# Second stage in another order of frequencies, its first sums taken early, and tile sums begun 11 steps ahead

## The chip, the cores and the metric

One core of a Trainium2 chip runs the whole kernel. The metric is the device time of one execution in microseconds (us). TensorE (PE) does matrix products; VectorE (DVE), ScalarE (ACT) and GpSimd (POOL) do elementwise work; SyncE (SP) and ACT issue the DMA transfers. Each engine works through its own instructions in program order.

## What is computed

The reference is a long convolution with a gate, followed by a two-layer network:

```python
h_filt = (np.maximum(pos_emb @ w1, 0.0) @ w2) * np.exp(-0.01 * pos)[:, None]
u = x * v                                   # (2, 12480, 128)
y = irfft(rfft(u, 2 * S) * rfft(h_filt, 2 * S))[:, :S]
t = (x * y).reshape(2 * S, 128)             # 24960 rows
h = t @ w_in                                # 128 -> 2048
out = np.maximum(0.01 * h, h) @ w_out       # 2048 -> 128
```

## The kernel before, in words

The convolution of length 12480 is a transform of 98 x 128 points, split in two: 98 "frequencies" k on one axis, 128 on the other. Batch entry 0 is transformed before the network begins; batch entry 1 is transformed in small portions (the generator `conv`) between the network's matrix products, during its first half.

**First stage (L230 to L384).** The products over the 98-long axis, written to `scr1`. Its last turn also fills `bin0`, the input of the first chunk of the second stage: `early` takes what lies in `scr1` already, `direct` copies the last rows from one on-chip tile to another.

**Second stage (loop at L717).** 25 chunks of 4 frequencies (the last has 2, since 98 = 24 x 4 + 2), in rising order of frequency. For chunk c: `load_b` (L612) brings its input two chunks ahead; PE makes the spectrum of the filter (`hidden`, L693) and of the input (`fwd`, L121); DVE and POOL multiply them (`product`, L124); PE transforms back (`back_halves`, L149); `evac` (L705) copies the result to `ct` and ACT's queue stores it to the scratch `scr2[0]`. On the way the weights are converted and split, and `fetch_a` loads inputs for batch 1 at chunks 20 and 23 (`FETCH`).

**Tiles.** The result is taken up in 64 tiles (32 for each batch entry). For tile t, `load_gx` (L538) loads a matrix `gt` and the gate's inputs `xm`, and `load_c` (L556) loads `cin` from `scr2`: in column block j = 0 the frequencies 0 to 48, in j = 1 the frequencies 49 to 97, real part in the lower 49 partitions and imaginary part in the upper 49; block j = 2 holds the upper frequencies again with real and imaginary parts exchanged. `join` (L593) makes four sums and differences of these in `cp`, by two operations of 512 columns (`cq`, L601) and four of 256 (`cp`, L604). It runs on POOL for all tiles but tile 0, which runs on DVE. There is one `cp` buffer and one `cq` buffer. For tile 0, `load_c` runs when chunk 24 begins; the last two chunks' results are not read back from `scr2` but copied from `ct` straight into `cin` by `last_c` (L575), 20 small transfers in SP's queue.

**Network (loop at the end of the function).** 50 blocks of up to 512 columns, each with 16 steps, 800 steps in all. A step i is six matrix products: three in `m1` (L837 to L839) and three in `m2` (L869 to L871) of three steps earlier. Between steps stands what the table `steps` says. Tile t has a step `ends[t]`; `front(t)` (L804) is called twice: 3 steps before `ends[t]`, when PE multiplies `gt` with `cp` (L810, 16 products into `yp`), and at `ends[t]`, when PE transposes (L818), ACT rounds (`zh`, L829) and POOL subtracts (`zl`, L830). The block in which the tile's columns begin needs `zh` and `zl` in its first step. The due times come from

```python
for t in reversed(range(1, total)):
    e = min(e - 8, first[t] * NF - 3)
    ends[t] = e
```

so two tiles follow each other at 16 steps (tile 32 at 24, tile 1 stands at step 5) or, where two begin in the same block, at 8 steps. Worked out from this, 30 tiles come 8 steps after the one before; with t at least 36 there are 14 of them: 36, 37, 40, 41, 44, 45, 48, 49, 52, 53, 57, 58, 61 and 62; tile 33 is one more, and 15 lie between tile 2 and tile 31. Tiles 35, 39, 43, 47, 51, 56 and 60 come 16 steps after their predecessor and 8 before their successor; they reach `ends[t]` only three steps before their block begins. `join(t)` stands at `ends[t] - 8` in program order. `load_tile(t)` stands one step after `ends[t - 2]`. Batch 1's transform is spread over the steps up to 375.

Of the kernel before, what the change touches and what calls it, by code (L numbers as in the profile page):

```python
# [22 lines left out]
KC = 4  # L23
# [7 lines left out]
def tile_conv_mlp(ctx, tc, x, v, pos_emb, w1, w2, w_in, w_out, cf, cr, cg, cb, ci, cw, out):  # L31
# [6 lines left out]
    NCH = (NA + KC - 1) // KC  # L38
    R0 = 96
    L, H = slice(0, HB), slice(HB, 2 * HB)  # L40

    const = ctx.enter_context(tc.tile_pool(name="const", bufs=1))
    dram = ctx.enter_context(tc.tile_pool(name="dram", bufs=1, space=bass.MemoryType.DRAM))
# [163 lines left out]
    with tc.manual_schedule():  # L207
# [22 lines left out]
        with ExitStack() as st:  # L230
# [64 lines left out]

            NC0 = HB // MC
            DIR, EARLY = 1, 1
            load_pos(0)
            nc.vector.memset(w1bd, 0.0)
            for i in range(2):  # L300
# [10 lines left out]
            for c in range(NC0):  # L311
# [40 lines left out]
                def early():  # L352
                    for ri in range(2):
                        rows = slice(HB * ri, HB * ri + HB - DIR * MC)
                        nc.sync.dma_start(out=bin0[rows], in_=scr1[rows, :KC, :].rearrange("p k (s e) -> p k s e", s=2))
# [200 lines left out]
        def load_c(t):  # L556
            b, mp = divmod(t, NT)
            ci_t = mlp.tile([NA, 3, 2, 2, D], F32, tag="cin", name="cin")
            n = KH if t else (NCH - 2) * KC - KH
            ms = slice(2 * mp, 2 * mp + 2)  # L560
            for r in range(2):
                if t:
                    nc.sync.dma_start(out=ci_t[KH * r:KH * r + KH, 0:2].rearrange("k j m s d -> k j (m s d)"),
                                      in_=scr2[b][:, r, ms, :].rearrange("(j k) m e -> k j (m e)", j=2))
                else:
                    for j, k1 in ((0, KH), (1, n)):
                        nc.sync.dma_start(out=ci_t[KH * r:KH * r + k1, j].rearrange("k m s d -> k (m s d)"),
                                          in_=scr2[b][KH * j:KH * j + k1, r, ms, :].rearrange("k m e -> k (m e)"))
            nc.sync.dma_start(out=ci_t[KH:KH + n, 2].rearrange("k m s d -> k (m s d)"),
                              in_=scr2[b][KH:KH + n, 0, ms, :].rearrange("k m e -> k (m e)"))  # L570
            for i in range(2):
                nc.sync.dma_start(out=ci_t[:n, 2, :, i, :], in_=scr2[b][KH:KH + n, 1, ms, D - D * i:2 * D - D * i])
            ld[t] = (ci_t, *ld[t][1:])

        def last_c(ct, k0, n):  # L575

            ci_t = ld[0][0]
            k0 -= KH
            for r in range(2):
                for m in range(2):  # L580
                    src = ct[HB * r + m:HB * r + m + 1, :n]
                    nc.sync.dma_start(out=ci_t[KH * r + k0:KH * r + k0 + n, 1, m], in_=src)
                    if r == 0:
                        nc.sync.dma_start(out=ci_t[KH + k0:KH + k0 + n, 2, m], in_=src)
                    else:
                        for i in range(2):
                            nc.sync.dma_start(out=ci_t[k0:k0 + n, 2, m, i], in_=src[:, :, 1 - i])

        def load_tile(t):
            load_gx(t)  # L590
            load_c(t)

        def join(t):  # L593
# [11 lines left out]
            ld[t] = (cp, g, xt)  # L605

        with ExitStack() as st:
            sbb = st.enter_context(tc.tile_pool(name="sbb", bufs=2, reuse_waits="tile"))
# [65 lines left out]
            bins[0] = bin0  # L674
            load_b(1)
            wprep = weights()
            FETCH = [NCH - 5, NCH - 2]
            late = []
# [26 lines left out]
            def evac(c):  # L705
                ct = sbb.tile([128, KC, 2, D], F32, tag="ct", name="ct", bufs=2)
                k0, n = chunk(c)
                run(back_evac(dps.pop(c), ct, n))
                if c >= NCH - 2:
                    last_c(ct, k0, n)  # L710
                store_back(0, c, ct, nc.scalar)

            eh, dps = {}, {}
            ahead(A0)
            next(conv)
            hidden(0)
            for c in range(NCH):  # L717
                if c + 2 < NCH:
                    load_b(c + 2)
                if c == NCH - 2:  # L720
                    load_gx(0)
# [5 lines left out]
                if c == NCH - 2:  # L727
                    mult_a(1)
                for f in late:
                    f()  # L730
                late = []
                n = chunk(c)[1]
                t, es = bins.pop(c), eh.pop(c)
                hp = two("h")
                for ri in range(2):
                    for k in range(n):
                        i, j = 64 * (k % 2), ri * n // 2 + k // 2
                        nc.tensor.matmul(hp[k % 2][:, D * j:D * j + D], es[i:i + 64, k // 2, ri, :], w22[i:i + 64, :],
                                         start=True, stop=True)
                hs = sbb.tile([128, 2, KC // 2, 2, D], F32, tag="hs", name="hs", bufs=2)  # L740
                for i in range(2):
                    nc.scalar.copy(hs[:, :, :n // 2, i, :],
                                   hp[i][:, :n * D].rearrange("p (r j d) -> p r j d", r=2, d=D))
# [5 lines left out]
                if c + 1 < NCH:  # L749
                    hidden(c + 1)  # L750
# [4 lines left out]
                product(ab, up, hs, n * D, pins[c], nc.vector if c >= NCH - 2 else nc.gpsimd)  # L755
                if c >= 1:
                    dps[c - 1] = two("d")
                    back_halves(dps[c - 1], pins.pop(c - 1), c - 1)
                    evac(c - 1)
                for _ in range(2):  # L760
                    next(wprep, None)

# [3 lines left out]
                late.clear()  # L766

            ahead(A1)
            dps[NCH - 1] = two("d")
            back_halves(dps[NCH - 1], pins.pop(NCH - 1), NCH - 1)  # L770
            evac(NCH - 1)
            load_c(1)
            mult_a(2)
            ahead(A2)
# [170 lines left out]
        SLOTS = ends[NT] - 14  # L945
        done = AHEAD
        frt = front(0)
        join(0)
        next(frt)
        for _ in range(4 * A4):  # L950
            next(conv)
# [100 lines left out]
```

## Time and profile before

| | us |
|---|---|
| median of 3 runs (lowest, highest) | 1816.6 (1814.48, 1820.26) |
| the profiled execution's own time | 1818.74 |
| its span in the trace | 1816.9 |
| PE busy | 1695.9 (93% of the span) |
| DVE busy | 1122.9 (62%) |
| ACT busy | 986.7 (54%) |
| POOL busy | 793.7 (44%) |

The stages in this execution: first stage to about 168 us, second stage to about 345 us, then the start of the network; batch 1's transform runs beside the network until about 1140 us; from there to the end the network runs alone. A busy share says little by itself: what ended each idle time of PE, and the clock that PE was granted (PEclk, 1.00 is 2.4 GHz and 0.50 is 1.2 GHz), are to be read by stage.

### The profile page before, as it was taken

The page shows a single profiled execution, that of the slowest core. Times are in us where ns is not written, and L with a number is a line of the kernel's source. Part 1 is how long each engine was busy: PE and PEld are TensorE (multiplying, and loading weights), DVE is VectorE, ACT ScalarE, POOL GpSimd, SP SyncE. Part 2 cuts the span into 40 slices and gives each one's busy share as a digit, 9 for nine tenths or more (in the row PEclk, how much of TensorE's full clock was granted, in tenths as well). Part 3 has the DMA queues.
Part 4 walks back from the last instruction along what each step waited for, and adds up shares of the span by engine and source line. Part 5 has one row for each costly group of instructions (what it writes and reads, how often), then busy time and mean ns, then how long its engine had stood idle before and what let it go on. Part 6 is the DMA issues. An engine that isn't in the chain of part 4 may idle for free.

```text
span 1816.9 us, 27218 instructions
## 1 busy us (share of the span) xinstructions
PE 1695.9 (93%) x9185; PEld 1342.0 (74%) x9185; DVE 1122.9 (62%) x1702; ACT 986.7 (54%) x2006; POOL 793.7 (44%) x732
## 2 busy tenths in 40 slices
PE   6787999469999999999999999999999999999998
PEld 6786555268888877787887778777777777777778
DVE  4575788534554555554555554667767776777775
ACT  1222455224444466676666665556565666665656
POOL 3453112134424367776767673433424333425330
PEclk9889999769999999999999999999999999999999
DMA  9898999464666466565666622121211122111110
GB/s 226 241 282 251 320 324 336 163 169 135 196 179 186 121 163 174 151 182 147 184 162 172 169 77 88 54 66 42 68 55 53 53 60 68 47 50 58 52 31 19
DMA packets 165788, 253.26 MB, mean 139 GB/s; under 512 B 13730, under 2 KB 118458, under 8 KB 162576
## 3 DMA queue, kind: packets, MB, share of 16 engines
q1 hardware_dynamic: 145504, 225.82, 43.9%
q10 hardware_dynamic: 20144, 25.69, 4.0%
q8 instruction: 73, 1.20, 0.3%
q14 instruction: 67, 0.55, 0.1%
HBM read 167.94 MB, written 83.43 MB: 138 GB/s over the span
## 4 chain that ended last, share of the span: by engine, by line
PE 50%; DMA 13%; DVE 11%; issue 10%; POOL 8%; SPq 4%; ACT 3%; ACTq 0%; POOLq 0%; DVEq 0%
PE mh L837 6%; PE acc L870 6%; PE acc L871 6%; PE mh L839 6%; PE mh L838 6%; PE acc L869 6%; POOL cp L604 4%; DVE rl L854 3%; POOL cq L601 3%; PE cv L135 3%; PE yp L810 2%; DMA scr<-o 2%; PE cv L405 2%; DMA ft<-in_cf_dram 2%; DMA cin<-scr 2%
## 5 line engine op out<-in xcount | busy, mean ns | idle before, releaser
L844 DVE SCALAR_TENSOR_TENSOR rl<-mh,rh 128x512 fp32r<-128x512 f32 (+2 forms) x400 | 269.3, 677 | 323.5 <-ACT rh L843 320.4
L854 DVE TENSOR_TENSOR rl<-r,rh 128x512 fp32r<-128x512 f32 (+1 forms) x400 | 348.0, 885 | 148.5 <-ACT rh L853 141.6
L849 ACT ACTIVATE r<-mh 128x512 f32<-128x512 f32 (+1 forms) x400 | 235.3, 588 | 213.6 <-PE mh L839 196.7
L843 ACT ACTIVATE rh<-mh 128x512 fp32r<-128x512 f32 (+2 forms) x400 | 234.7, 590 | 202.3 <-PE mh L839 185.5
L837 PE MATMUL mh<-zh,w_in_h 128*128 128x512 f32 (+3 forms) x800 | 333.6, 417 | 2.8 <-DVE rl L844 1.5
L870 PE MATMUL acc<-rl,w_out_h 128*128 128x512 f32 (+3 forms) x800 | 317.9, 397 | 5.8 <-DVE rl L854 5.7
L838 PE MATMUL mh<-zl,w_in_h 128*128 128x512 f32 (+3 forms) x800 | 316.0, 395 | 0.0
L839 PE MATMUL mh<-zh,w_in_l 128*128 128x512 f32 (+3 forms) x800 | 316.0, 395 | 0.0
L869 PE MATMUL acc<-rh,w_out_h 128*128 128x512 f32 (+3 forms) x800 | 315.4, 394 | 0.0
L871 PE MATMUL acc<-rh,w_out_l 128*128 128x512 f32 (+3 forms) x800 | 314.4, 393 | 0.0
L830 POOL TENSOR_TENSOR zl<-zf,zh 128x390 fp32r<-128x390 f32 (+24 forms) x110 | 67.9, 632 | 541.0 <-ACT zh L829 382.3
L604 POOL TENSOR_TENSOR cp<-cq 98x256 f32<-98x256 f32 x252 | 216.1, 878 | 9.9
L601 POOL TENSOR_TENSOR cq<-cin 98x512 f32<-98x512 f32 x126 | 176.7, 1402 | 65.9 <-DMA cin<-scr 61.0
L870 PEld LDWEIGHTS acc<-rl,w_out_h 128*128 128x128 f32 x800 | 152.7, 191 | 51.6 <-DVE rl L854 18.8
L837 PEld LDWEIGHTS mh<-zh,w_in_h 128*128 128x128 f32 x800 | 153.0, 191 | 39.3 <-issue 9.3
L839 PEld LDWEIGHTS mh<-zh,w_in_l 128*128 128x128 f32 x800 | 153.1, 191 | 33.5
L869 PEld LDWEIGHTS acc<-rh,w_out_h 128*128 128x128 f32 x800 | 152.7, 191 | 34.0
L871 PEld LDWEIGHTS acc<-rh,w_out_l 128*128 128x128 f32 x800 | 152.7, 191 | 32.0
L838 PEld LDWEIGHTS mh<-zl,w_in_h 128*128 128x128 f32 x800 | 153.5, 192 | 25.5 <-DVE zl L830 0.4
L851 DVE CAST rh<-r 128x512 fp32r<-128x512 f32 (+1 forms) x200 | 115.7, 578 | 38.8 <-ACT r L849 36.0
L810 PE MATMUL yp<-cp,gt 98*64 98x128 f32 x1024 | 88.6, 289 | 53.5 <-issue 27.3
L810 PEld LDWEIGHTS yp<-cp,gt 98*64 98x64 f32 x1024 | 61.4, 141 | 87.8 <-issue 46.8
(151 smaller groups left out, 2351.2 us busy)
## 6 DMA issues: line engine op xcount, KB each, us to landing
cin<-scr SPq DMA_DIRECT2D x126, 196.0 KB
hd<-hspec SPq DMA_DIRECT2D x48, 512.0 KB
scr<-o SPq DMA_DIRECT2D x32, 588.0 KB
bin<-scr SPq DMA_DIRECT2D x23, 768.0 KB
scr1b<-o SPq DMA_DIRECT2D x32, 392.0 KB
hspec<-hs ACTq DMA_DIRECT2D x48, 256.0 KB
scr<-ct ACTq DMA_DIRECT2D x24, 512.0 KB
xm<-in_x_dram SPq DMA_DIRECT2D x128, 96.0 KB
```

Of the source, the lines that this page charges most:

```text
L601: eng.tensor_tensor(out=q, in0=src[:, :, :, 0, :], in1=src[:, :, :, 1, :], op=ALU.subtract if p else ALU.add)
L604: eng.tensor_tensor(out=cp[:, p, w], in0=q[:, 0], in1=q[:, 1], op=op)
L837: nc.tensor.matmul(hp, w_in_h[:, fs], zh, start=True, stop=False)
L838: nc.tensor.matmul(hp, w_in_h[:, fs], zl, start=False, stop=False)
L839: nc.tensor.matmul(hp, w_in_l[:, fs], zh, start=False, stop=True)
L843: nc.scalar.activation(out=rh, in_=hp, func=AF.Relu)
L844: nc.vector.scalar_tensor_tensor(out=rl, in0=hp, scalar=0.0, in1=rh, op0=ALU.max, op1=ALU.subtract)
L849: nc.scalar.activation(out=r, in_=hp, func=AF.Lrelu, alpha=0.01)
L854: nc.vector.tensor_tensor(out=rl, in0=r, in1=rh, op=ALU.subtract)
L869: nc.tensor.matmul(ap, w_out_h[:, f, :], rh, start=(f == 0 and at0[k] >= S), stop=False)
L870: nc.tensor.matmul(ap, w_out_h[:, f, :], rl, start=False, stop=False)
L871: nc.tensor.matmul(ap, w_out_l[:, f, :], rh, start=False, stop=(f == NF - 1))
```

## The change

1. The second stage takes chunks 13 to 24, then chunk 12 (which holds frequency 48 of the lower half and 49 to 51 of the upper), then chunks 0 to 11. `bin0` holds chunk 13.
2. Tile 0's `load_gx` and the load of the whole upper half (and frequency 48) stand at the stage's 17th turn instead of the 24th and 25th; its sums of the upper half (`join_hi`) stand on POOL at the 21st turn; `load_gx(1)` moves from the 25th to the 23rd turn. At the 25th turn frequencies 0 to 39 are loaded. `last_c` copies chunks 10 and 11, which are in the lower half: 8 small transfers.
3. For every tile, `cin` is loaded by half: seven transfers instead of five. The sums are split: two operations of 256 columns on the upper half, written to `cp`, then for each sign one of 256 columns on the lower half and two of 256 that combine, eight instead of six.
4. In the network, the sums of tile t stand at `ends[t] - 11` instead of `ends[t] - 8`, but for tiles 1, 32 and 33.

```diff
+    MID = KH // KC
+    ORD = [*range(MID + 1, NCH), MID, *range(MID)]
...
-                        nc.sync.dma_start(out=bin0[r0:r0 + 1], in_=o[:KC, ri, m])
+                        nc.sync.dma_start(out=bin0[r0:r0 + 1], in_=o[KB0:KB0 + KC, ri, m])
...
+        def rows_c(t, j, lo, hi):
...
+            ks = slice(KH * j + lo, KH * j + hi)
             for r in range(2):
...
+                nc.sync.dma_start(out=ci_t[KH * r + lo:KH * r + hi, j].rearrange("k m s d -> k (m s d)"),
+                                  in_=scr2[b][ks, r, ms, :].rearrange("k m e -> k (m e)"))
+            if j:
+                nc.sync.dma_start(out=ci_t[KH + lo:KH + hi, 2].rearrange("k m s d -> k (m s d)"),
+                                  in_=scr2[b][ks, 0, ms, :].rearrange("k m e -> k (m e)"))
+                for i in range(2):
+                    nc.sync.dma_start(out=ci_t[lo:hi, 2, :, i, :], in_=scr2[b][ks, 1, ms, D - D * i:2 * D - D * i])
...
+        def join_hi(t):
...
+            for p, op in ((0, ALU.add), (1, ALU.subtract)):
+                nc.gpsimd.tensor_tensor(out=cp[:, p, 1], in0=ci_t[:, 1 + p, :, 0, :], in1=ci_t[:, 1 + p, :, 1, :], op=op)
...
+        def join_lo(t):
...
             eng = nc.gpsimd if t else nc.vector
-            for p in range(2):
-                q = mlp.tile([NA, 2, 2, D], F32, tag="cq", name="cq", bufs=1)
-                src = ci_t[:, 0:2 + p:1 + p]
-                eng.tensor_tensor(out=q, in0=src[:, :, :, 0, :], in1=src[:, :, :, 1, :],
-                                  op=ALU.subtract if p else ALU.add)
+            for p, op in ((0, ALU.add), (1, ALU.subtract)):
+                eng.tensor_tensor(out=cq[:, p], in0=ci_t[:, 0, :, 0, :], in1=ci_t[:, 0, :, 1, :], op=op)
                 for w, op in ((0, ALU.add), (1, ALU.subtract)):
-                    eng.tensor_tensor(out=cp[:, p, w], in0=q[:, 0], in1=q[:, 1], op=op)
+                    eng.tensor_tensor(out=cp[:, p, w], in0=cq[:, p], in1=cp[:, p, 1], op=op)
...
-            hidden(0)
-            for c in range(NCH):
-                if c + 2 < NCH:
-                    load_b(c + 2)
-                if c == NCH - 2:
+            hidden(ORD[0])
+            for i, c in enumerate(ORD):
+                if i + 2 < NCH:
+                    load_b(ORD[i + 2])
+                if i == NCH - 9:
                     load_gx(0)
-                if c == NCH - 1:
                     load_c(0)
+                if i == NCH - 5:
+                    join_hi(0)
+                if i == NCH - 3:
                     load_gx(1)
-                if c in FETCH:
-                    fetch_a(1 + FETCH.index(c))
+                if i == NCH - 1:
+                    rows_c(0, 0, 0, (MID - 2) * KC)
+                if i in FETCH:
+                    fetch_a(1 + FETCH.index(i))
...
-            at(ends[t] - 8, "join", t)
+            at(ends[t] - (11 if t % NT > 1 else 8), "join", t)
...
-                join(t)
+                join_hi(t)
+                join_lo(t)
```

## Rows read from the trace of the kernel before

**Rows 1.** Waits: engine, line, what it waited for: us in total, times, longest.

```profile
PE yp L810 <- issue: 27.3, 1, 27.3
PE yp L810 <- POOL cp L604: 26.0, 38, 2.8
```

**Rows 2.** The same between 400 and 1140 us, by PE.

```profile
PE yp L810 <- POOL cp L604: 4.6, 9, 1.5
```

**Rows 3.** Stretches: start:end, length, busy time by engine, PEclk, DMA share, GB/s.

```profile
330.00:372.00 42.00, 13.59 (x100) 9.07 (x96) 15.46 (x28) 6.87 (x16) 2.53 (x1) 0.70 0.35 117
372.00:385.00 13.00, 11.41 (x55) 9.43 (x57) 5.72 (x11) 3.16 (x8) 5.68 (x6) 0.52 0.86 217
1150.00:1760.00 610.00, 585.58 (x2828) 453.65 (x2827) 441.75 (x563) 378.57 (x752) 231.52 (x230) 0.97 0.18 54
1302.00:1306.00 4.00, 3.93 (x14) 3.09 (x15) 2.76 (x5) 0.60 (x1) 0.01 (x1) 0.58 0.30 87
```

**Rows 4.** Timeline at the second stage's end: start, duration, engine, line, operation.

```profile
338.98 10.75 SPq L572 DMA_DIRECT2D cin<-scr  x2
...
343.10 0.65 ACT L203 COPY ct<-dp 128x256 f32<-128x256 f32 x2 [0.24 <-PE dp L149]
...
369.20 0.56 SPq L582 DMA_DIRECT2D cin<-ct  x1
369.81 1.16 SPq L587 DMA_DIRECT2D cin<-ct  x2
371.00 0.69 DVE L601 TENSOR_TENSOR cq<-cin 98x512 f32<-98x512 f32 x1 [11.61 <-DMA cin<-ct]
...
371.72 0.76 DVE L604 TENSOR_TENSOR cp<-cq 98x256 f32<-98x256 f32 x2
...
372.25 2.92 PE L810 MATMUL yp<-cp,gt 98*64 98x128 f32 x16 [27.26 <-issue]
```

**Rows 5.** A stretch of the same end, columns as in rows 3.

```profile
342.00:354.00 12.00, 2.99 (x25) 2.40 (x24) 1.45 (x3) 1.23 (x3) 0.00 (x0) 0.70 0.07 25
```

**Rows 6.** Timeline of the second stage: forward products of four chunks.

```profile
297.67 1.94 PE L121 MATMUL up<-bin,mb 128*64 128x512 f32 x8
...
303.30 1.94 PE L121 MATMUL up<-bin,mb 128*64 128x512 f32 x8
...
317.11 1.94 PE L121 MATMUL up<-bin,mb 128*64 128x512 f32 x8
...
326.18 3.49 PE L121 MATMUL up<-bin,mb 128*64 128x512 f32 x8
```

**Rows 7.** Timeline: the sums and the front of tile 41, 8 steps after tile 40.

```profile
1295.00 1.29 POOL L601 TENSOR_TENSOR cq<-cin 98x512 f32<-98x512 f32 x1
...
1299.60 0.66 PE L810 MATMUL yp<-cp,gt 98*64 98x128 f32 x8
...
1300.10 1.92 POOL L604 TENSOR_TENSOR cp<-cq 98x256 f32<-98x256 f32 x2
...
1302.07 0.65 PE L810 MATMUL yp<-cp,gt 98*64 98x128 f32 x6 [0.43 <-POOL cp L604]
```

**Rows 8.** Timeline: tile 39, which comes 16 steps after tile 38, and 8 before 40.

```profile
1271.54 1.10 PE L810 MATMUL yp<-cp,gt 98*64 98x128 f32 x16
...
1278.73 1.02 POOL L830 TENSOR_TENSOR zl<-zf,zh 128x342 fp32r<-128x342 f32 x2 [17.72 <-ACT zh L829]
...
1280.30 0.40 PE L838 MATMUL mh<-zl,w_in_h 128*128 128x512 f32 x1
```

**Rows 9.** One line's operations, all: duration in ns (min/median/max), first and last start.

```profile
L604 POOL TENSOR_TENSOR cp<-cq x252: 722/902/1252, 377.5 to 1757.4; 98x256 f32<-98x256 f32 x126
```

**Rows 10.** Timeline beside batch 1's transform: last load of tile 14, front of tile 13.

```profile
666.35 0.68 SPq L572 DMA_DIRECT2D cin<-scr  x2
...
673.57 0.66 PE L810 MATMUL yp<-cp,gt 98*64 98x128 f32 x6 [0.25 <-POOL cp L604]
```

**Rows 11.** The chain of waits: start, length, transfer.

```profile
1114.59 4.95 DMA cin<-scr
```

More of the change, by code (lines that the diff above doesn't have):

```diff
@@ L297, in tile_conv_mlp @@
             DIR, EARLY = 1, 1
+            KB0 = ORD[0] * KC
             load_pos(0)
@@ L354, in early @@
                         rows = slice(HB * ri, HB * ri + HB - DIR * MC)
-                        nc.sync.dma_start(out=bin0[rows], in_=scr1[rows, :KC, :].rearrange("p k (s e) -> p k s e", s=2))
+                        nc.sync.dma_start(out=bin0[rows], in_=scr1[rows, KB0:KB0 + KC, :].rearrange("p k (s e) -> p k s e", s=2))
                 def direct(m, o, c=c):
@@ L558, in load_c @@
             ci_t = mlp.tile([NA, 3, 2, 2, D], F32, tag="cin", name="cin")
-            n = KH if t else (NCH - 2) * KC - KH
+            ld[t] = (ci_t, *ld[t][1:])
+            rows_c(t, 1, 0, KH)
+            if t:
+                rows_c(t, 0, 0, KH)
+            else:
+                rows_c(t, 0, MID * KC, KH)
+        def rows_c(t, j, lo, hi):
+            b, mp = divmod(t, NT)
+            ci_t = ld[t][0]
             ms = slice(2 * mp, 2 * mp + 2)
+            ks = slice(KH * j + lo, KH * j + hi)
@@ L561, in load_c @@
             for r in range(2):
[L562 to L573, printed above, removed]
+                nc.sync.dma_start(out=ci_t[KH * r + lo:KH * r + hi, j].rearrange("k m s d -> k (m s d)"),
+                                  in_=scr2[b][ks, r, ms, :].rearrange("k m e -> k (m e)"))
@@ L575, in last_c @@
+            if j:
[3 more added lines that the diff above has]
+                    nc.sync.dma_start(out=ci_t[lo:hi, 2, :, i, :], in_=scr2[b][ks, 1, ms, D - D * i:2 * D - D * i])
         def last_c(ct, k0, n):
-            ci_t = ld[0][0]
-            k0 -= KH
             for r in range(2):
                 for m in range(2):
[L581 to L587, printed above, removed]
+                    nc.sync.dma_start(out=ld[0][0][KH * r + k0:KH * r + k0 + n, 0, m],
+                                      in_=ct[HB * r + m:HB * r + m + 1, :n])
@@ L591, in load_tile @@
             load_c(t)
-        def join(t):
+        def join_hi(t):
             ci_t, g, xt = ld[t]
             cp = mlp.tile([NA, 2, 2, 2, D], F32, tag="cp", name="cp", bufs=1)
-            eng = nc.gpsimd if t else nc.vector
-            for p in range(2):
-                q = mlp.tile([NA, 2, 2, D], F32, tag="cq", name="cq", bufs=1)
-                src = ci_t[:, 0:2 + p:1 + p]
-                eng.tensor_tensor(out=q, in0=src[:, :, :, 0, :], in1=src[:, :, :, 1, :],
-                                  op=ALU.subtract if p else ALU.add)
+            for p, op in ((0, ALU.add), (1, ALU.subtract)):
+                nc.gpsimd.tensor_tensor(out=cp[:, p, 1], in0=ci_t[:, 1 + p, :, 0, :], in1=ci_t[:, 1 + p, :, 1, :], op=op)
+            ld[t] = ci_t, g, xt, cp
+        def join_lo(t):
+            ci_t, g, xt, cp = ld[t]
+            cq = mlp.tile([NA, 2, 2, D], F32, tag="cq", name="cq", bufs=1)
+            eng = nc.gpsimd if t else nc.vector
+            for p, op in ((0, ALU.add), (1, ALU.subtract)):
+                eng.tensor_tensor(out=cq[:, p], in0=ci_t[:, 0, :, 0, :], in1=ci_t[:, 0, :, 1, :], op=op)
                 for w, op in ((0, ALU.add), (1, ALU.subtract)):
-                    eng.tensor_tensor(out=cp[:, p, w], in0=q[:, 0], in1=q[:, 1], op=op)
-            ld[t] = (cp, g, xt)
+                    eng.tensor_tensor(out=cp[:, p, w], in0=cq[:, p], in1=cp[:, p, 1], op=op)
+            ld[t] = cp, g, xt
         with ExitStack() as st:
@@ L672, in weights @@
                 nc.vector.tensor_tensor(out=wc_l, in0=wcs, in1=wc_h, op=ALU.subtract)
-            bins[0] = bin0
-            load_b(1)
+            bins[ORD[0]] = bin0
+            load_b(ORD[1])
             wprep = weights()
@@ L708, in evac @@
                 run(back_evac(dps.pop(c), ct, n))
-                if c >= NCH - 2:
+                if c in ORD[-2:]:
                     last_c(ct, k0, n)
@@ L715, in tile_conv_mlp @@
             next(conv)
-            hidden(0)
-            for c in range(NCH):
-                if c + 2 < NCH:
-                    load_b(c + 2)
-                if c == NCH - 2:
+            hidden(ORD[0])
[3 more added lines that the diff above has]
+                if i == NCH - 9:
                     load_gx(0)
-                if c == NCH - 1:
                     load_c(0)
+                if i == NCH - 5:
+                    join_hi(0)
+                if i == NCH - 3:
                     load_gx(1)
-                if c in FETCH:
-                    fetch_a(1 + FETCH.index(c))
-                if c == NCH - 2:
+                if i == NCH - 1:
+                    rows_c(0, 0, 0, (MID - 2) * KC)
+                if i in FETCH:
+                    fetch_a(1 + FETCH.index(i))
+                if i == NCH - 2:
                     mult_a(1)
@@ L736, in tile_conv_mlp @@
                     for k in range(n):
-                        i, j = 64 * (k % 2), ri * n // 2 + k // 2
-                        nc.tensor.matmul(hp[k % 2][:, D * j:D * j + D], es[i:i + 64, k // 2, ri, :], w22[i:i + 64, :],
+                        h, j = 64 * (k % 2), ri * n // 2 + k // 2
+                        nc.tensor.matmul(hp[k % 2][:, D * j:D * j + D], es[h:h + 64, k // 2, ri, :], w22[h:h + 64, :],
                                          start=True, stop=True)
                 hs = sbb.tile([128, 2, KC // 2, 2, D], F32, tag="hs", name="hs", bufs=2)
-                for i in range(2):
-                    nc.scalar.copy(hs[:, :, :n // 2, i, :],
-                                   hp[i][:, :n * D].rearrange("p (r j d) -> p r j d", r=2, d=D))
+                for k in range(2):
+                    nc.scalar.copy(hs[:, :, :n // 2, k, :],
+                                   hp[k][:, :n * D].rearrange("p (r j d) -> p r j d", r=2, d=D))
                 hs = hs.rearrange("p r j i d -> p r (j i d)")
@@ L748, in tile_conv_mlp @@
                     nc.scalar.dma_start(out=hspec[c][:, :, s, :n * D], in_=hs[HB * s:HB * s + HB, :, :n * D])
-                if c + 1 < NCH:
-                    hidden(c + 1)
+                if i + 1 < NCH:
+                    hidden(ORD[i + 1])
                 for _ in range(3):
@@ L754, in tile_conv_mlp @@
                 ab = [sbb.tile([128, 2, 512], F32, tag=g, name=g) for g in ("ta", "tb")]
[L755 to L759, printed above, removed]
+                product(ab, up, hs, n * D, pins[c], nc.vector if i >= NCH - 2 else nc.gpsimd)
+                if i >= 1:
+                    b4 = ORD[i - 1]
+                    dps[b4] = two("d")
+                    back_halves(dps[b4], pins.pop(b4), b4)
+                    evac(b4)
                 for _ in range(2):
@@ L768, in tile_conv_mlp @@
             ahead(A1)
-            dps[NCH - 1] = two("d")
-            back_halves(dps[NCH - 1], pins.pop(NCH - 1), NCH - 1)
-            evac(NCH - 1)
+            dps[ORD[-1]] = two("d")
+            back_halves(dps[ORD[-1]], pins.pop(ORD[-1]), ORD[-1])
+            evac(ORD[-1])
             load_c(1)
@@ L947, in tile_conv_mlp @@
         frt = front(0)
-        join(0)
+        join_lo(0)
         next(frt)
```

## The prediction

> **What bounds the kernel now.** I read the waits first, PE's, because PE is busy 93% of the span: the question is which of its idle times this change touches. Two rows stand out, both waits of a tile's first products, L810 [rows 1]. One is a single gap of 27.3 us. The other is 26.0 us in 38 pieces, all on POOL's sums; only 4.6 us of these lie between 400 and 1140 us, where batch 1's transform fills PE [rows 2]. Then I read stretches [rows 3]. Between 330 and 372 us PE is busy 13.59 of 42 us, and the 13 us behind it run at a mean granted clock of 0.52. From 1150 to 1760 us PE is idle 24.4 of 610 us and the mean clock is 0.97. So there are two places: the seam at 345 to 385 us, and the last third.
>
> The seam: the second stage's last result leaves ACT at 343.75 us, and L810 starts at 372.25 [rows 4]. Between them SP works off a queue: two loads L572 alone hold it for 10.75 us, `load_gx(1)` and the 20 small copies of `last_c` follow, and DVE begins the sums at 371.00. While SP is stuck, the DMA engines are busy 0.07 of the time [rows 5], near 1/16, as if one of the 16 did all the work.
>
> The last third: tile 41's front runs from 1299.60 to 1302.72, 3.12 us [rows 7]; tile 39's takes 1.10 [rows 8]. The difference, 2.0 us, is the wait for sums that began at 1295.00 and end at 1302.02 [rows 7]. Tiles at a distance of 16 steps show no such wait, since POOL takes up their sums as soon as its queue is free, far ahead of need. The 14 tiles at a distance of 8 do: their sums stand behind the previous tile's `zl`, five steps before the front. After tile 41's front PE runs on at 0.58 over 4 us, mostly at the lower level of 1.2 GHz [rows 3].
>
> **The change, part by part.** The sum is made against the profiled execution, 1818.7 us (span 1816.9); the median of the runs is 2.1 us below it.
>
> *The seam.* The 20 copies become 8, four of them behind the last chunk; the long loads and both `load_gx` leave the end. The last chunk has 4 frequencies instead of 2, but the short one is still in the stage, so ACT's last copy moves little: I take 344.3. Four copies at a pitch of 0.61 (369.20 to 369.81) put the last start at 346.1. From the start of such a copy to DVE's start are 1.80 us (369.20 to 371.00), so DVE starts at 347.9. Two operations of 256 columns at 0.38 (0.76 for two) and a little slack give 348.8 for L810 [rows 4]: **23.4 us earlier**. If each copy took three times as long, it would be 20. The low clock behind a gap of some 4 us instead of 27 should end sooner: over 13 us at 0.52 PE loses 6 us [rows 3], and I take **1.5** of it back (bounds 0 and 4).
>
> *The price in the second stage.* At its 17th turn 13 more transfers (`load_gx` and `load_c`) stand in SP's queue, ahead of the next `load_b` and of the weights, on which PE, DVE and the turns behind wait. The nearest row is the turn that now holds `load_gx(0)` and a `fetch_a`, 13 transfers too: the next forward products come 9.07 us after the last (317.11 to 326.18) instead of 5.63 (297.67 to 303.30) [rows 6], 3.4 us more. That turn gets lighter, since `load_gx(0)` leaves it; the 23rd gets `load_gx(1)`. I take **3 us lost**; bounds 0 (cover by the input chunks loaded two ahead) and 10 (three such turns). `join_hi(0)` is two POOL operations of 0.72 us [rows 9], in front of POOL's half of a product; its load was issued four turns, 22 us, before. The new order, `bin0`, and DVE's six operations in place of six cost nothing, the work is the same.
>
> *The last third, gain.* With 11 steps the sums of a tile at distance 8 stand at the previous tile's front, ahead of its `zl`. They may start when that front has released `cp`, some 7 us sooner, and end some 4 us ahead of need: 14 x 2.0 = **28 us** of waiting go. (The idle time in the stretch is lower, since pipelined products count as busy.) The low clock goes with them: 0.03 of 610 us [rows 3] is 18.3 us, 15 to 21 with the rounding; I take **15.5**.
>
> *The last third, price.* POOL now does the previous tile's `zl` behind the new sums. For the 7 tiles like 39 that is tight: its front ends at 1272.64, and the block needs `zl` at 1280.30, 7.66 us later [rows 8]. The six operations took 7.02 us [rows 7]. Eight of 256 columns replace each 512-column one (1.29 us) by two of 0.72 [rows 7, 9], 0.15 more each: 7.3, say 7.4. The first piece of `zl` adds 0.9 (342 of 390 columns, 1.02 for both pieces), so `zl` is ready 8.3 to 8.7 us after the front: 1 us of stall, **7 us lost**. Bounds: at 0.722 each the sums take about 6.1 and nothing stalls; at 1.252 each they take 10, 3.4 us a tile, 24 in all. I add **3 us** for two falls of the clock (0.42 of 4 us, 1.7 each [rows 3]).
> A rule of the Trainium skill speaks against the early place (GPSIMD Engine Reference, Key points): GpSimd shares its SBUF interfaces with VectorE and contends with VectorE instructions that have two SBUF inputs, which L854 has. The trace agrees in so far as L604 takes 0.96 us in tile 41 (1.92 for two) and 0.722 at least. Were all eight operations slowed, the sums would take 7.7 us and the price would be 9 instead of 7.
>
> *Beside batch 1's transform (385 to 1140 us).* The same two effects: of the 4.6 us of waiting [rows 2] about 3.5 go. Against it POOL's `zl` and its operations for batch 1 stand behind the sums at 15 tiles; the transform's products between the steps leave PE more time there. I take **0**; bounds 5 gained, 8 lost (half a microsecond a tile).
>
> *Two more transfers and two more POOL instructions a tile.* An issue takes SP 0.34 us (0.68 for two [rows 10]), and SP loads a tile ahead; POOL is busy 232 of 610 us late [rows 3]. Covered; without cover it would be 1 us a tile.
>
> Sum: 23.4 + 1.5 - 3 + 28 + 15.5 - 7 - 3 = 55.4. 1818.7 - 55.4 = 1763.3; against the median, 1761. I say **1763**.
>
> **The rivals.**
> - *The seam gains little* (12%). The 13 transfers hold each other up and delay `load_b` and the weights, 10 us; `fetch_a` ahead of the small copies takes another 10. Then 1783. For it: the turn of 9.07 us [rows 6]. Against it: at the seam the DMA engines are idle [rows 5].
> - *The stall moves instead of going* (16%). `zl` comes 3.4 us late at each of the 7 tight tiles, with a fall of the clock (1.7): 36 us in place of 10, so 29 are won in all, and 1789; beside the transform it may take 5 to 8 more: 1795. It decides at sums of over 6.7 us (7.66 less 0.9); the present ones take 7.02 [rows 7, 8].
> - *Everything comes off* (12%). No stall for `zl`, no fall of the clock, 4 more beside the transform: 1747.
> - *Slower: POOL stands before a `cin` that has not landed* (6%). Beside the transform the sums now come up at the previous front. Tile 14's last load is issued by 667.03 and, at 4.95 us, lands at 672.0; tile 13's front ends at 674.23: a margin of 2.2 us [rows 10, 11]. If loads land later than that (seven transfers, a busier SP), POOL waits with batch 1's products behind it, and PE behind them. At 4.4 us and a fall of the clock (1.7) for 15 tiles, 91 us would go: 1816.6 - 55 + 91 = 1853.
> - *It doesn't do what it says* (3%). If the one `cp`, or `cin`, holds the sums back and not their place, and another wait takes the seam's place, 1816. That all these waits are on POOL's L604 [rows 1] speaks against it.
>
> **How the numbers follow.** The forecast has the remaining 51%. The range, 1745 to 1796, holds the first four cases but for their extremes, and leaves out the last two. A measurement of this kernel can tell about 0.3% (5 us) from no change. Faster takes the first four: 0.91. Same: 0.03. Slower: 0.06.
>
> **What the profile after would show.** Right: L810's single gap falls from 27.3 to some 4 us and its first start from 372 to about 352; `last_c` has 8 issues; the waits of L810 on POOL nearly vanish and the fronts of the 14 tiles take 1.10 us; the clock is 1.00 from 1150 us on; L838 waits for `zl` at 7 tiles, near 1 us. Wrong: forward products at the 17th to 20th turn further apart than 9 us; POOL waiting for `cin` beside the transform; L838 waiting over 2 us; a clock that still falls in the last third.

## The result, and the profile after

The changed kernel takes 1755.1 us (median; 1750.3 to 1757.7) beside 1816.9 for the kernel before on the same chip: a ratio of 0.966, with a 95% interval of 0.963 to 0.968. The forecast was 1763, in a range of 1745 to 1796. The profiled execution took 1754.5 us, its span is 1752.7, 64.2 us shorter than before.

In the changed kernel the lines have moved: L810 is L822, L830 is L842, L837 to L839 are L849 to L851, L854 is L866, L121 is L123; L604's place is taken by L600 (upper half), L609 (`cq`) and L611 (`cp`).

PE's waits over the whole run, which answer to [rows 1] and [rows 2] (line, what it waited for: us in total, times, longest):

```profile
PE yp L822 <- POOL cp L611: 7.0, 6, 4.6
PE yp L822 <- issue: 6.6, 1, 6.6
PE mh L850 <- POOL zl L842: 6.2, 8, 1.0
```

The gap of 27.3 us is 6.6, the 26.0 us of waits for sums are 7.0, 4.6 of them at one tile. A new wait stands beside them, for `zl`, eight times and at most 1.0 us each. Stretches of the same execution (columns as in [rows 3]); the third is in the second stage:

```profile
1150.00:1760.00 610.00, 592.18 (x3039) 476.41 (x3037) 449.36 (x611) 401.12 (x811) 252.18 (x285) 1.00 0.18 55
...
345.00:356.00 11.00, 7.34 (x56) 5.76 (x55) 6.49 (x11) 4.07 (x8) 0.00 (x0) 0.97 0.63 201
...
200.00:335.00 135.00, 122.37 (x1018) 70.88 (x1016) 109.54 (x236) 64.67 (x132) 30.94 (x24) 0.99 0.99 319
```

From 1150 us on the granted clock is 1.00 (0.97 before), and at the seam the DMA engines are busy 0.63 of the time.

To see where 64.2 us come from I cut the run at instructions that both kernels have, by their starts in the timeline: the *stage* from the third to the last (25th) group of forward products of the second stage; the *seam* from there to step 0 of the network; *beside* from step 0 to step 432, while the transform runs; *alone* from step 432 to 799. What lies ahead of the stage differs by up to 4 us between executions of the same code.

| one execution each, us | stage | seam | beside | alone |
|---|---|---|---|---|
| before | 141.1 | 46.3 | 816.5 | 611.3 |
| after | 144.3 | 26.9 | 810.5 | 566.8 |
| gain | -3.2 | 19.4 | 6.0 | 44.5 |

These make 66.7; 2.5 us were lost ahead of the stage, where the change only fills `bin0` with other rows (the run of the steps alone, below, has the old code there and loses 2.8).

### The profile page after: what moved, and what is told of

It is laid out like the page before. It is cut to its first block, busy times and chain, and to the rows that moved or that the text cites. A ratio compares the mean times of both kernels' runs of the same rounds, so it can differ in the third digit from the quotient of the medians.

```text
span 1752.7 us, 27421 instructions
## 1 busy us (share of the span) xinstructions
PE 1666.5 (95%) x9185; PEld 1331.7 (76%) x9185; DVE 1112.9 (63%) x1702; ACT 984.4 (56%) x2006; POOL 828.7 (47%) x860
## 5 line engine op out<-in xcount | busy, mean ns | idle before, releaser
L866 DVE TENSOR_TENSOR rl<-r,rh 128x512 fp32r<-128x512 f32 (+1 forms) x400 | 326.2, 828 | 124.6 <-ACT rh L865 117.5
L849 PE MATMUL mh<-zh,w_in_h 128*128 128x512 f32 (+3 forms) x800 | 330.4, 413 | 2.1 <-ACT zh L841 1.3
L851 PE MATMUL mh<-zh,w_in_l 128*128 128x512 f32 (+3 forms) x800 | 312.6, 391 | 0.0
L882 PE MATMUL acc<-rl,w_out_h 128*128 128x512 f32 (+3 forms) x800 | 312.1, 390 | 0.0
L611 POOL TENSOR_TENSOR cp<-cq,cp 98x256 f32<-98x256 f32 x252 | 218.6, 867 | 19.8
L842 POOL TENSOR_TENSOR zl<-zf,zh 128x390 fp32r<-128x390 f32 (+24 forms) x110 | 72.3, 670 | 317.1 <-ACT zh L841 194.0
L600 POOL TENSOR_TENSOR cp<-cin 98x256 f32<-98x256 f32 x128 | 103.4, 828 | 202.7 <-PE yp L822 122.9
L849 PEld LDWEIGHTS mh<-zh,w_in_h 128*128 128x128 f32 x800 | 151.1, 189 | 37.6 <-issue 7.6
L851 PEld LDWEIGHTS mh<-zh,w_in_l 128*128 128x128 f32 x800 | 151.0, 189 | 32.5
L863 DVE CAST rh<-r 128x512 fp32r<-128x512 f32 (+1 forms) x200 | 126.7, 634 | 28.6 <-ACT r L861 25.3
L865 ACT CAST rh<-r 128x512 fp32r<-128x512 f32 (+1 forms) x200 | 121.9, 610 | 6.4
L609 POOL TENSOR_TENSOR cq<-cin 98x256 f32<-98x256 f32 x126 | 104.7, 831 | 2.1 <-DMA cin<-scr 2.1
```

The costliest lines, as they stand in the source:

```text
L611: eng.tensor_tensor(out=cp[:, p, w], in0=cq[:, p], in1=cp[:, p, 1], op=op)
L849: nc.tensor.matmul(hp, w_in_h[:, fs], zh, start=True, stop=False)
L851: nc.tensor.matmul(hp, w_in_l[:, fs], zh, start=False, stop=True)
L863: nc.vector.tensor_copy(rh, r)
L866: nc.vector.tensor_tensor(out=rl, in0=r, in1=rh, op=ALU.subtract)
L882: nc.tensor.matmul(ap, w_out_h[:, f, :], rl, start=False, stop=False)
```

## The experiments

"The mark" in the expectations is the changed kernel, run once more. All the runs in one table, before the reasons (cut as above; one profiled execution each, the ratio from repeated runs beside the kernel before):

| run | us | ratio to before | stage | seam | beside | alone |
|---|---|---|---|---|---|---|
| the mark | 1754.0 | 0.964 (0.962 to 0.967) | 143.2 | 26.8 | 809.1 | 566.8 |
| steps alone | 1773.2 | 0.975 (0.972 to 0.977) | 141.7 | 45.9 | 809.2 | 569.6 |
| all but the steps | 1824.1 | 1.002 (1.000 to 1.004) | 143.7 | 26.8 | 821.0 | 628.3 |
| undivided sums | 1756.2 | 0.965 (0.963 to 0.968) | 146.0 | 27.0 | 811.8 | 569.4 |
| `zl` on DVE | 1751.5 | 0.962 (0.960 to 0.963) | 146.4 | 26.9 | 811.4 | 561.6 |
| sums cut in two | 1756.9 | 0.966 (0.964 to 0.967) | 144.8 | 26.7 | 809.0 | 571.8 |
| copies first | 1753.1 | 0.963 (0.961 to 0.964) | 143.9 | 23.3 | 811.5 | 566.8 |
| `load_gx(1)` at turn 19 | 1760.2 | 0.966 (0.964 to 0.969) | 150.6 | 29.0 | 809.1 | 566.8 |
| `load_gx(1)` at turn 25 | 1757.5 | 0.966 (0.963 to 0.969) | 148.8 | 28.4 | 809.6 | 566.8 |
| tile 2 behind the front | 1754.4 | 0.965 (0.962 to 0.968) | 144.8 | 28.4 | 809.8 | 566.8 |
| tile 2 behind the products | 1746.9 | 0.962 (0.959 to 0.964) | 144.8 | 27.1 | 803.2 | 566.8 |
| three edits together | 1741.4 | 0.956 (0.954 to 0.959) | 146.8 | 25.2 | 805.2 | 561.5 |

Where the network runs alone, executions of the same code agree within 0.1 us, so half a microsecond can be told there, while the whole run spreads by 6 us in the mark and by up to 10 in the others.

**The mark.** No edit.

> The changed kernel once more, as the mark for the runs beside it: near 1755 us, 0.965 to 0.968 of the kernel before. Its spread says what difference between two variants can be told.

The time is as expected (1750.6 to 1756.4 us), the ratio a little lower.

**Steps alone.** The kernel before, with one line of the change:

```diff
-            at(ends[t] - 8, "join", t)
+            at(ends[t] - (11 if t % NT > 1 else 8), "join", t)
```

> The kernel before with one number changed: sums begun 11 steps ahead of need instead of 8, still undivided, and the old order of the second stage. Theory (the place of the sums makes the last third's gain): the fronts of the tiles at a distance of 8 steps take 1.10 us and the clock stays up, so 33 to 40 us go, 1777 to 1784 us; no gain at the seam; PE's waits for rl behind the second layer's products stay (about 6 us on PE after 1150 us), and the stall at zl is 5 to 8 us. Rival (dividing the sums into 256-column operations is what makes the place good: undivided they take 7.0 us or more and zl comes late): zl stalls of 10 us or more in all, falls of the clock remain, under 20 us gained, 1797 us or more.

Measured 1773.2 us: 47 us come from one number, more than the theory's 40. Alone the network gains 41.7 us and beside the transform 7.3, where I had expected nothing. PE's waits there, from 1150 to 1740 us:

```profile
PE acc L870 <- DVE rl L854: 5.8, 16, 0.5
```

The waits for `rl` stay, as the theory says; of the 5 to 8 us of waits for `zl` that it also named there are none (why, the run of the undivided sums shows).

**All but the steps.** The changed kernel with the sums back at 8 steps:

```diff
-            at(ends[t] - (11 if t % NT > 1 else 8), "join", t)
+            at(ends[t] - 8, "join", t)
```

> The changed kernel with the sums back at 8 steps: the new second stage and the divided sums without the new place. Theory: only the seam's gain of 12 to 14 us is left, 1800 to 1806 us; in the last third the fronts wait 1.5 to 2.5 us again with falls of the clock, and L822 waits some 25 us for POOL as before. Rival (dividing the sums shortens them, so that half of the last third's gain comes from that): 1780 to 1790 us.

Both were wrong: 1824.1 us, slower than before if anything. The seam and the stage give what they gave, 16.9 us together, and all of it goes again: 4.5 us beside the transform and 17.0 alone. POOL from 1287 us, the sums of a tile 8 steps behind the one before, and PE's waits of that execution:

```profile
1287.81 1.89 POOL L600 TENSOR_TENSOR cp<-cin 98x256 f32<-98x256 f32 x2
1289.66 0.92 POOL L609 TENSOR_TENSOR cq<-cin 98x256 f32<-98x256 f32 x1
1290.66 2.21 POOL L611 TENSOR_TENSOR cp<-cq,cp 98x256 f32<-98x256 f32 x2
1292.83 0.91 POOL L609 TENSOR_TENSOR cq<-cin 98x256 f32<-98x256 f32 x1
1293.82 2.18 POOL L611 TENSOR_TENSOR cp<-cq,cp 98x256 f32<-98x256 f32 x2
```

```profile
PE yp L822 <- POOL cp L611: 39.0, 45, 3.4
```

Eight operations take 8.2 us where six took 7.02 [rows 7], and in the old place PE waits for what they take longer: 39.0 us instead of 26.0 [rows 1]. With more low clock behind the longer waits (0.95 from 1150 to 1760 us, 0.97 before) that is the loss. Dividing the sums is no gain by itself; the new place is what lets the kernel afford it.

**Undivided sums.** The changed kernel, with the old `join` in the new place from tile 1 on:

```diff
-                join_hi(t)
-                join_lo(t)
+                join(t)
```

> The changed kernel with the six undivided sums per tile from tile 1 on, in the new place. Theory (the division frees VectorE: two 512-column operations hold it up longer than the short ones): PE's waits for rl return, about 6 us, and the time is 1759 to 1763 us. Rival (the place and the steady clock took those waits away, the division nothing): 1752 to 1757 us, no waits for rl, and the stall at zl is 5.7 us or less, since six operations take less time than eight.

1756.2 us, not to be told from the mark, and both theories are half right: the waits for `rl` return in full and those for `zl` go, 2.6 us more in the stretch alone. PE's wait from 1150 to 1740 us:

```profile
PE acc L895 <- DVE rl L879: 5.3, 15, 0.4
```

`zl` is in time because the first of the six operations writes `cq` and needn't wait for `cp`: POOL does it ahead of the previous tile's front, and only the five others stand behind that front and ahead of `zl`. At tile 39 they take 5.3 us; the eight of the changed kernel, of which the first two write `cp`, take 7.3 there (its rows are shown further down).

```profile
1247.45 1.45 POOL L624 TENSOR_TENSOR cp<-cq 98x256 f32<-98x256 f32 x2 [10.12 <-PE yp L835]
1248.97 1.47 POOL L621 TENSOR_TENSOR cq<-cin 98x512 f32<-98x512 f32 x1
1250.52 2.21 POOL L624 TENSOR_TENSOR cp<-cq 98x256 f32<-98x256 f32 x2
1253.38 1.24 POOL L855 TENSOR_TENSOR zl<-zf,zh 128x342 fp32r<-128x342 f32 x2 [0.66 <-ACT zh L854]
```

POOL and DVE in the timeline of this execution, an operation of 512 columns and what runs before and beside it:

```profile
1280.13 1.29 POOL L621 TENSOR_TENSOR cq<-cin 98x512 f32<-98x512 f32 x1
...
1278.19 0.69 DVE L879 TENSOR_TENSOR rl<-r,rh 128x512 fp32r<-128x512 f32 x1
1280.54 1.43 DVE L879 TENSOR_TENSOR rl<-r,rh 128x512 fp32r<-128x512 f32 x1 [1.66 <-ACT rh L878]
```

DVE in the changed kernel, beside operations of 256 columns (tile 39's, shown further down):

```profile
1246.63 0.69 DVE L866 TENSOR_TENSOR rl<-r,rh 128x512 fp32r<-128x512 f32 x1 [0.90 <-ACT rh L865]
1248.61 1.00 DVE L863 CAST rh<-r 128x512 fp32r<-128x512 f32 x1 [0.68 <-ACT r L861]
1249.64 2.26 DVE L866 TENSOR_TENSOR rl<-r,rh 128x512 fp32r<-128x512 f32 x2
```

In these rows the same DVE operation takes 0.69 us by itself, 1.13 beside short POOL operations and 1.43 beside a long one. With the two runs before, the stretch alone is a square of four: old place 611.3 undivided and 628.3 divided, new place 569.5 and 566.8. The place is worth 42 to 62 us; the division costs 17 in the one and gives 3 in the other.

**`zl` on DVE** for the seven tight tiles (39 and those like it):

```diff
-                (nc.gpsimd if t else nc.vector).tensor_tensor(...)
+                (nc.gpsimd if t and t not in tight else nc.vector).tensor_tensor(...)
```

> The changed kernel with zl of the seven tight tiles (39 and those like it) on VectorE instead of POOL. Theory (the sums ahead of zl on POOL's queue are what makes it late): PE's wait for zl, 6.2 us in 8 pieces in the mark, is gone; 5 to 7 us faster than the mark's 1754.0 us, 1747 to 1749 us. Rival (VectorE is then late with rl or r behind it, so that the wait only changes its name): 1753 to 1757 us, with waits for rl of some 6 us on PE.

Alone 561.6 us, 5.2 less than the mark and the least of the runs with one edit: from 1150 to 1740 us the list of PE's waits is empty, and what is left of `zl` is a wait of PE's weight loads:

```profile
PEld mh L850 <- DVE zl L842: 3.6, 7, 0.6
```

So the theory's place is shown. The whole run gains less, 1751.5 us, between the theory's 1747 to 1749 and the rival's times, and the interval overlaps the mark's; in the profiled execution (1748.1) the stage was 3.2 us and the part beside the transform 2.3 us longer than the mark's.

**Sums cut in two.**

```diff
-            at(ends[t] - (11 if t % NT > 1 else 8), "join", t)
+            at(ends[t] - (11 if t % NT > 1 else 8), "high", t)
+            at(ends[t] - 8, "low", t)
```

> The changed kernel with the sums cut in two: the two of the upper half 11 steps ahead, the six others 8 steps ahead, with zl between them on POOL. Theory (all of a tile's sums must stand ahead of zl): the waits for zl go, but six operations of 0.96 to 1.0 us, some 6 us, begun behind zl end 1 us or more late, where the undivided ones of 7.02 us ended 2.0 us late; 14 fronts wait again, with falls of the clock, 1762 to 1780 us. Rival (what had to go is only the first 2 us of sums): no front waits, no zl waits, 1747 to 1751 us.

Neither: 1756.9 us. Waits for `zl` are gone, and fourteen fronts wait again, but by far less than the theory had it:

```profile
PE yp L822 <- POOL cp L611: 5.8, 14, 0.4
```

The clock stays at 1.00. Beside the 561.6 us of a stretch with neither wait, this costs 10.2 us, 0.73 a front.

**Copies first.**

```diff
-        A0, A1, A2, A3, A4, A5 = 2, 2, 0, 1, 1, 0
+        A0, A1, A2, A3, A4, A5 = 2, 1, 1, 1, 1, 0
```

> The changed kernel with one batch of the transform's first stage, and its store to scratch, moved behind the last small copies of the second stage. Theory (the copies at the seam take 1.1 to 1.2 us each instead of 0.61 because that store is ahead of them and its data are still being moved): four copies in 2.5 us, L822 starts 2 to 4 us earlier, 1750 to 1752 us. Rival (the copies are slow by themselves, a partition of 2 KB to 4 others each): L822 starts where it did, or the gap of PE, 6.3 us, grows by the work moved out of it, 1754 to 1758 us.

The theory holds for the copies, which stand together now and take 0.79 us each, and the gap of PE falls to 3.1 us:

```profile
343.71 6.35 SPq L588 DMA_DIRECT2D cin<-ct  x8
```

The seam is 3.5 us shorter, and 2.4 come back beside the transform, where the batch that was moved now stands. In all 1753.1 us, no difference that can be told.

**`load_gx(1)` earlier, and later.** From `i == NCH - 3` to `i == NCH - 7` (turn 19), and to `i == NCH - 1` (turn 25):

> The changed kernel with the input loads of tile 1 issued at the 19th turn of the second stage instead of the 23rd. Theory (at the 23rd they stand in SP's queue between the loads on which the last turns wait, which costs the last four turns about 3 us): the last turns are 5.6 to 7.5 us apart instead of up to 10.3, the stage ends 2 to 4 us earlier, 1750 to 1752 us. Rival (the price moves with the loads to the 19th turn, where two loads of the same kind come close together): the stage ends where it did, 1753 to 1756 us.

> The changed kernel with the input loads of tile 1 issued at the last turn of the second stage instead of the 23rd. Theory (these six transfers, 3 to 6 us of them on SP, hold up the queues on which a turn's loads and stores go: at the 23rd turn ACT stood 4 us before its store of hs, at the 19th the price was 7 us or more; behind the last load of bin nothing waits for SP until 340.7): the turns at the end are 5.6 to 7.5 us apart, the first L822 comes 2 to 4 us earlier against the last L123 of the turn before, 1750 to 1752 us. Rival (they then hold up the last copies, or tile 1's front at its fifth step, by as much): 1753 to 1758 us.

Neither gained. The first is beyond both theories; the second has the rival's time, but not for its reason. In both it is the stage that is long, 150.6 and 148.8 us, more than in any other run. With the old order it was 141.1 and 141.7, with the new one 143.2 to 146.8 in ten executions (144.9 in the mean): the price of the new order is some 3.5 us, and no place of these six transfers takes it away.

The rows say where it is paid: from the 17th to the 19th group of forward products, at the turn that got the 13 transfers and the next, it is 12.0 us in both executions with the old order and 14.3 to 17.6 in all twelve with the new one. PE waits there for `es`, a copy that ACT makes on the way to the filter's spectrum (`hs`). In the changed kernel ACT takes 3.47 us over the issue of two stores of `hs` while SP issues the loads of `cin` (1.17 one turn earlier), `es` stands behind them in ACT's queue, and PE waits for it:

```profile
284.34 3.47 ACTq L759 DMA_DIRECT2D hspec<-hs  x2
287.86 0.58 ACT L710 COPY es<-ep 128x512 f32<-128x512 f32 x1 [4.17 <-DMA hspec<-hs]
288.49 1.16 PE L749 MATMUL hp<-w,es 64*128 64x128 f32 x16 [2.81 <-ACT es L710]
```

Why the stores are held up isn't shown. One candidate is the load on the DMA engines. The stretch of the stage before, and the idle one behind it:

```profile
200.00:335.00 135.00, 127.50 (x1046) 72.32 (x1046) 113.68 (x240) 67.27 (x137) 28.89 (x22) 0.99 0.99 325
...
345.00:356.00 11.00, 0.00 (x0) 0.00 (x0) 0.00 (x0) 0.00 (x0) 0.00 (x0) 0.59 0.16 52
```

They were 0.99 busy already, and the change moves into that stretch what lay in the idle one: `load_gx(1)` (2 x 75, 2 x 96 and 3 KB) and the upper half of `cin` (3 x 98 and 2 x 49 KB), 0.74 MB, which at 320 GB/s are 2.3 us, an estimate. That this is the cause isn't shown, and one row speaks against it: between 280 and 300 us, where the time is lost, the DMA engines of the changed kernel are 0.93 busy, less than the 1.00 before. To tell, it would take a run that leaves out those bytes. Before, then after:

```profile
280.00:300.00 20.00, 19.78 (x170) 11.30 (x168) 17.43 (x40) 10.58 (x21) 3.83 (x3) 1.00 1.00 330
```

```profile
280.00:300.00 20.00, 16.80 (x146) 9.57 (x144) 14.45 (x33) 9.40 (x19) 3.73 (x3) 1.00 0.93 309
```

The Trainium skill (DMA: Bandwidth & Descriptors, Issuing engines are not separate DMA queues) says that all DMAs share 16 engines whoever issues them, so that issuing on several engines at once saves only the time to issue. No run here tries another engine's queue.

**Tile 2's loads earlier.** First `load_tile(2)` right behind `run(frt)`, tile 0's whole front; then right behind `next(frt)`, its products:

> The changed kernel with the loads of tile 2 issued right behind tile 0's front instead of at the first step. Theory (the wait of 4.2 us left in tile 2's front, and the low clock for the 8 us behind it, come from its cin, which lands at 380 to 382 us because SP issues the loads at 371.6 to 377.2 behind four fetches and a store; POOL and the place of the sums have no part in it): the front takes 1.10 us, the clock does not fall at 384, 6 to 8 us gained, 1746 to 1748 us. Rival (the loads wait for the buffers of tile 0 and hold the fetches behind them on SP, so that the transform runs dry and PE waits for xv): the front's wait is 2 us or more, or PE waits for the first stage, 1752 to 1760 us.

> The changed kernel with the loads of tile 2 issued as soon as tile 0's products are done with its buffers, ahead of the next fetch and of the store of the transform (behind the front's end, in the run before, they stood in the same place of SP's queue as in the mark, 15 us after the first L822). Theory (tile 2's front waits for its cin alone): its loads start at about 361 us instead of 371.6, the front's 4.2 us become 1.10 and the low clock behind it goes, 6 to 8 us gained, 1746 to 1748 us. Rival (the fetch that now stands behind them comes 6 us later, and the transform's products with it, so that PE stays at the low clock through the first steps): 1752 to 1758 us.

The first changed nothing: the loads kept their place on SP, behind the same store, and began 15.9 us after the first L822 (15.3 in the mark). The second is what the theory asked for, 1746.9 us. The stretch behind tile 2's front, in the changed kernel and in this run:

```profile
383.00:395.00 12.00, 7.95 (x35) 6.38 (x36) 1.82 (x3) 1.36 (x3) 8.30 (x9) 0.72 0.38 115
```

```profile
383.00:395.00 12.00, 12.00 (x73) 11.37 (x72) 5.74 (x10) 6.24 (x15) 8.24 (x11) 1.00 0.56 179
```

**Three edits together.** `zl` on DVE, copies first, tile 2 behind the products:

> Three of the edits together: tile 2's loads right behind tile 0's products, zl of the seven tight tiles on VectorE, and the last copies of the second stage ahead of one batch of the transform and its store. Theory (they act at different places and add up: about 7 us at tile 2, 5 at zl, 0 to 3 at the copies): 1740 to 1744 us, below both kernels. Rival (at the seam the batch moved behind the copies meets the loads moved ahead of it, and the two spoil each other): 1745 to 1752 us.

1741.4 us, 0.956 (0.954 to 0.959) of the kernel before: the theory's value, and the least of all. By the cut, one execution each, the gains against the mark add up alone (5.2 us) and beside the transform (3.9 us: tile 2's 5.9 less the 2.4 that the moved batch costs there); at the seam 1.6 are left of the copies' 3.5. PE's longest waits from 355 us on:

```profile
PE yp L822 <- POOL cp L611: 3.2, 6, 0.8
PE yp L822 <- issue: 3.1, 1, 3.1
PE mh L849 <- ACT zh L841: 1.3, 1, 1.3
```

## Why the prediction was right

The places were right, the sum (55.4 us; measured 64.2) was low by what follows. That it is no further off is in part luck: 5.5 us less at the seam (its clock term counted in) and 2.5 lost ahead of the stage stand against 11 more in the last third and 6 more beside the transform.

*The seam, predicted 23.4, measured 19.1* (L810 or L822 against the last forward products: 37.7 us before, 18.6 after; I had 14.2). The end of it in the changed kernel:

```profile
350.46 1.07 ACT L205 COPY ct<-dp 128x512 f32<-128x512 f32 x2 [0.81 <-PE dp L151]
350.99 0.83 SPq L421 DMA_DIRECT2D scr1b<-o  x2
351.92 4.67 SPq L588 DMA_DIRECT2D cin<-ct  x4
357.92 0.43 DVE L609 TENSOR_TENSOR cq<-cin 98x256 f32<-98x256 f32 x1 [3.63 <-DMA cin<-ct]
358.90 2.78 PE L822 MATMUL yp<-cp,gt 98*64 98x128 f32 x16 [6.56 <-issue]
```

ACT's last copy ends 11.2 us after the last forward products, where I took 9.7: the full last chunk costs more than I gave it. From there to L822 it is 7.4 us and not 4.5, because a copy took 1.17 us and not the 0.61 of [rows 4]; I had left room for that ("three times as long"). Copied ahead of the store L421 they take 0.79. The 1.5 us of clock behind the gap didn't come: from L822 to step 0 are 8.3 us, 8.6 before, and the 16 steps behind it take 1.7 longer, with tile 2's front still late. That front I had not looked at.

*The second stage, predicted 3, measured 3.2* (3.5 in the mean of the runs). The size, taken from the row of another turn [rows 6], and the turn were right: 3.2 us are lost from the 17th to the 19th group of forward products. The wait was another one: not for `load_b` or the weights, but for `es` behind ACT's stores. What holds those up stays open, and two moves of transfers in SP's queue made the stage longer. The sign that I named, more than 9 us between two groups there, didn't show in this execution (8.6 at most), but did in five of the others (9.4 to 10.1).

*The last third's gain, predicted 28 and 15.5.* The 14 fronts took 43.5 us before and take 15.4, 28.2 less. Before, nine falls of the clock, each some 3.4 us at 0.50, take 1.7 us of full clock apiece, 15.4 in all; after, no stretch from 1150 to 1740 us has a low clock. Both terms are right.

*Its price, predicted 7 and 3, measured 5.7 and 0.* Tile 39, to be laid beside [rows 8], in the timelines of POOL and of PE:

```profile
1247.19 1.44 POOL L600 TENSOR_TENSOR cp<-cin 98x256 f32<-98x256 f32 x2 [9.63 <-PE yp L822]
1248.59 0.73 POOL L609 TENSOR_TENSOR cq<-cin 98x256 f32<-98x256 f32 x1
1249.40 1.95 POOL L611 TENSOR_TENSOR cp<-cq,cp 98x256 f32<-98x256 f32 x2
1251.31 1.18 POOL L609 TENSOR_TENSOR cq<-cin 98x256 f32<-98x256 f32 x1
1252.57 1.95 POOL L611 TENSOR_TENSOR cp<-cq,cp 98x256 f32<-98x256 f32 x2
1254.48 1.69 POOL L842 TENSOR_TENSOR zl<-zf,zh 128x342 fp32r<-128x342 f32 x2
```

```profile
1245.95 1.10 PE L822 MATMUL yp<-cp,gt 98*64 98x128 f32 x16
...
1255.82 0.50 PE L850 MATMUL mh<-zl,w_in_h 128*128 128x512 f32 x1 [0.94 <-POOL zl L842]
```

The front ends at 1247.05, the sums take 7.3 us (forecast 7.4), and the product starts 8.8 us behind the front (I had `zl` ready at 8.3 to 8.7), having waited 0.94. That POOL's queue is the cause is shown by `zl` on DVE, which gives 5.2 back. The clock didn't fall behind such a wait.

*Not in the sum.* PE's waits for `rl` before (5.4 us, in 15 pieces, from 1150 to 1740 us) went with the long POOL operations; I had read DVE's contention as POOL's loss only. This and the falls that didn't come make 5.4 + 3 of the 11 us by which the last third was better than 33.5; 1.3 are the smaller price of `zl`, 1.3 I can't assign.
The rule that I weighed (the Trainium skill, GPSIMD Engine Reference, Key points) is borne out on both sides: L866 has two SBUF inputs, and it slows down as POOL does. In the trace the cast L863, with one input, slows down too, from 0.43 us to 1.00 in its row at 1248.61 us, which the part of the rule that I weighed doesn't cover.

*Beside the transform, predicted 0, measured 6.0.* Waits for sums went as expected, and the price for POOL's other work that I set against it doesn't show. The rival by which POOL stands before `cin` didn't come: from tile 3 to tile 31 no front waits. Tile 33, which the change leaves at 8 steps, still waits 2.0 us.

Of the rivals, "everything comes off" was nearest in time and in two of its three terms: no fall of the clock, and 6.0 us beside the transform where it had 4; the stall it left out came. (Its 1747 goes by the median; by the profiled execution, as the other sums, it is 1749.) The condition of "the stall moves" was met (sums of 7.3 us against 6.7), but the stall was 0.94 us a tile and not 3.4. Even the 8.2 us that the sums take in the old place would make it only some 1.9, an estimate; for 3.4 they'd have to take about 10.

## What to carry to other kernels

Where work on a side engine ends just late, look first at its place in the queue: one number gave 47 us here, of the 66 between the kernel before and the mark, while the division of the same work cost 17 us in the old place and gave 3 in the new. So test two parts of a change as a square of four, not each by itself against the end. And moving transfers from an idle stretch into a full one has a price, some 3.5 us here, paid where 13 of them stand; whether it is for their bytes or for the queues they hold up, these runs don't show.

## What the runs showed of the hardware

- A wait of PE of 0.94 us (for `zl`) or 0.43 (two pieces of a front) left the granted clock at 1.00; of the 14 fronts of 3.0 to 3.5 us in the kernel before, with some 2.0 of waiting, nine were followed by some 3.4 us at 0.50 (1.2 GHz) and five (tiles 36, 40, 44, 49 and 61) by none (read in stretches of 1 us).
- DVE's cast `rh`, with one input, takes 0.43 us by itself and 0.96 to 1.00 beside POOL's sums; L866 takes 0.69, 1.13 or 1.43 by the length of the POOL operation beside it (in the undivided sums 1.6 in the median beside operations of 512 columns); and POOL's 256 columns go from 0.72 to some 0.97 (1.95 for two), its 512 from 1.29 to 1.63. Each side pays.
- The issue of a small copy held SP 0.56 to 0.69 us in the kernel before, but 0.77 and 1.27 just behind the store L418; in the changed one 0.68 (2.73 for four) ahead of the store L421 and 1.17 behind it.
